# One load per chunk and two heads side by side in the rows of the array, in a fused retention and mixture-of-experts kernel

## The chip, the cores and the metric

The kernel runs on one core of a Trainium2 chip. The metric is the device time of one execution in microseconds (us); of several runs the median is given. Everything is read from one execution that the hardware profiler recorded. The engines are PE (TensorE, with PEld for its weight loads), DVE (VectorE), ACT (ScalarE), POOL (GpSimd) and SP (SyncE, which here issues the plain DMAs).

## The reference

Retention (a linear attention with a decaying state) over batch 4, 8 heads, 768 positions, head size 64, and behind it a mixture of 8 experts with top-1 routing over 3072 tokens of 512 features:

```python
for t in range(S):
    state = gamma * state + einsum('bhd,bhe->bhde', k[:, :, t], v[:, :, t])
    y[:, :, t] = scale * einsum('bhd,bhde->bhe', q[:, :, t], state)
x = y.transpose(0, 2, 1, 3).reshape(B * S, H * D)
logits = x @ w_gate;  expert_idx = argmax(logits);  gate_w = softmax(logits)[expert_idx]
for e in range(E):
    out[expert_idx == e] = gate_w * (relu(x @ w1[e]) @ w2[e])
```

## The kernel before

**Chunks.** The retention is computed in 24 chunks of 128 positions (6 per batch element), all eight heads at once, as four pairs of heads. For chunk `g` the kernel forms scores (key chunk times query chunk, masked to be causal), the output within the chunk (scores times values) and the carried part (queries times the state accumulated up to the chunk before). The decay is moved onto the operands: values are scaled by `cv` (negative powers of gamma), and queries or results by the table `G` (positive powers). The loop over `g` is written out in program order, one engine queue each, with no scheduler; only semaphores between engines hold things up.

**One pass of the loop** issues, in this order: `scores(g+1)`, `carry(g)`, `scale(g+2)`, for chunks 9 to 17 pieces of `split` (the weights of expert 0 cut into a high and a low part, ACT line 133, DVE or POOL line 134), `logits` of an earlier pair of chunks, `update(g)`, one or two stages of the routing of the batch element before (`gating`: `choose`, `soft`, `rank`, `slots`, `onehots`, `table`, `put_ids`, `weights`, `put_weights`), `output(g)`, the loads for chunk `g+4`, the store of a pair of chunks, and in four places a 1 MB weight load (`fetch`, line 125).

- `scale` (lines 207 to 215), POOL: from chunk 6 on, the queries times `G` in place (line 210); for every chunk the values times `cv` (line 212). For chunks below 6 `G` for that chunk is still being built (line 489, POOL, once per pass), and the result is multiplied instead (line 267, DVE).
- `scores` (217 to 226), PE line 222: for each half `h2` (the even or the odd head of the pairs) and each pair `p`, one matmul over all 128 rows. The moving operand holds the two heads' queries in the two row halves; the stationary operand `kt` holds one head's transposed keys in its row half and zeros in the other. So eight 128-row matmuls make the scores of eight heads, 64 rows of each being zeros. DVE line 224 masks the result into `Sb`, once per half.
- `carry` (244 to 250), PE line 249: four 128-row matmuls with the state of two heads as a block diagonal in `ub` (zeros off it).
- `update` (228 to 242), PE line 237: eight matmuls of 64 output rows each into the two halves of the partitions; ACT line 242 copies the state into `ub`, in two copies for the two diagonal blocks.
- `output` (252 to 272), PE line 257: eight matmuls, each 64 columns wide on the array, alternating between the two column halves. Then ACT line 269 copies `Y` to `xT` (DVE line 267 for chunks below 6), and DVE line 271 transposes it to `xn` for the store.
- `load` and `load_k` (193 to 202), SP: the three parts q, v, k of a chunk in one DMA of 768 KB, and the transposed keys as two DMAs of 128 KB, each into one row half of `kt`. `ld` has four buffers, `kts` four tiles; the loads of chunk `g+4` go where chunk `g` was.

**After the retention** PE computes an early half of expert 0 (`early_half`, `fill`), then all experts in `moe_main`. `L` (logits) has a PSUM bank of its own, `Y` one, the scores two.

A load in the program has this form, and the chunk's parts lie in memory as q, v, k and transposed k:

```python
nc.sync.dma_start(out=kts[g % 4][half[i], i], in_=qkv[g][half[i], 3].rearrange("a (p t) -> a p t", p=NP))
```

Of the kernel before, what the change touches and what calls it, by code (L numbers as in the profile page):

```python
# [43 lines left out]
G6 = CPB  # L44
BIG = 1 << 20
# [49 lines left out]
def retention_moe(ctx, tc, qkv, wg, w1, w2, cst, gdec, ustr, out):  # L95
# [75 lines left out]
    with ExitStack() as actx:  # L171
        apool = lambda name, bufs, **kw: actx.enter_context(tc.tile_pool(name=name, bufs=bufs, **kw))
        ld = apool("ld", 4)
# [10 lines left out]
        ubs = [ubp.tile([P, NP, P], F32, name=f"ub{i}") for i in range(3)]  # L184
        kts = [ubp.tile([P, 2, NP, C], F32, name=f"kt{i}") for i in range(4)]
# [3 lines left out]
        RAW = CPB  # L189
# [3 lines left out]
        def load(g, *parts):  # L193
            if g not in qs:
                qs[g] = ld.tile([P, 3, DM], F32, name="qkv_t", tag="ld")
            for part in parts or (slice(0, 3),):
                nc.sync.dma_start(out=qs[g][:, part], in_=qkv[g][:, part])

        def load_k(g):
            for i in range(2):  # L200
                nc.sync.dma_start(out=kts[g % 4][half[i], i],
                                  in_=qkv[g][half[i], 3].rearrange("a (p t) -> a p t", p=NP))

        def q_(g):
            return qs[g][:, 0].rearrange("a (p t) -> a p t", p=NP)

        def scale(g):
            c = g % CPB
            if g >= RAW:
                nc.gpsimd.tensor_tensor(out=q_(g), in0=q_(g), in1=G[:, c], op=ALU.mult)  # L210
            vs = wk.tile([P, H, D], F32, name="vs", bufs=3)
            nc.gpsimd.tensor_tensor(  # L212
                out=vs, in0=qs[g][:, 1].rearrange("a (h d) -> a h d", d=D),
# [3 lines left out]
        def scores(g):  # L217
            Sb = wk.tile([P, 2, NP, C], F32, name="Sb")
            for h2 in range(2):
                sp = ps_s.tile([P, NP, C], F32, name="sp")  # L220
                for p in range(NP):
                    nc.tensor.matmul(out=sp[:, p, :], lhsT=kts[g % 4][:, h2, p, :], rhs=q_(g)[:, p, :],  # L222
                                     start=True, stop=True)
                nc.vector.tensor_tensor(out=Sb[:, h2], in0=sp,
                                        in1=causal.unsqueeze(1).broadcast_to([P, NP, C]), op=ALU.mult)
            Sbs[g] = Sb

        def update(g):
# [4 lines left out]
            kn = qs[g][:, 2]  # L233
            for p in range(NP):
                for h2 in range(2):
                    r = slice(h2 * D, (h2 + 1) * D)
                    nc.tensor.matmul(out=U[r, p, :], lhsT=kn[:, p * P + h2 * D:p * P + h2 * D + D],
                                     rhs=vp[:, p, r], start=(c == 0 and p == 0), stop=True, skip_group_check=True)
            ub = ubs[g % 3]
            for h2 in range(2):  # L240
                r = slice(h2 * D, (h2 + 1) * D)
                nc.scalar.copy(out=ub[r, :, r], in_=U[r, :, :])

        def carry(g):
            c = g % CPB
            Y = Ys[g] = ps_1.tile([P, NP, C], F32, name="Y", tag="Y")
            if c > 0:
                for p in range(NP):
                    nc.tensor.matmul(out=Y[:, p, :], lhsT=ubs[(g - 1) % 3][:, p, :], rhs=q_(g)[:, p, :],
                                     start=(p == 0), stop=False, skip_group_check=True)  # L250

        def output(g):
            c = g % CPB
            Y, vp, Sb = Ys[g], vss[g], Sbs[g]
            for p in range(NP):
                for h2 in range(2):
                    nc.tensor.matmul(out=Y[h2 * D:(h2 + 1) * D, p, :],
                                     lhsT=vp[:, p, h2 * D:(h2 + 1) * D], rhs=Sb[:, h2, p, :],
                                     start=(c == 0 and p == 0), stop=True, skip_group_check=True)
# [6 lines left out]
            if g < RAW:  # L266
                nc.vector.tensor_tensor(out=xT, in0=Y, in1=G[:, c], op=ALU.mult)
            else:
# [747 lines left out]
```

## Time and profile before

| what | value |
|---|---|
| three runs | 447.74, 450.02, 451.33 us; median 450.02 |
| profiled execution, span from the first to the last instruction | 447.8 us |
| busy over the span | PE 419.0, DVE 284.4, ACT 148.0, POOL 293.0 us |
| mean granted PE clock | 0.979 of full speed |
| retention (up to the end of the last `output`) | 140.5 us |
| moved by DMA | 79.68 MB, of it 27.71 MB from 10 to 100 us |

The time of the profiled execution outside its span was not recorded for it; the span alone lies at the lowest of the three runs. The views used further on are: a table of busy time per engine in chosen stretches (with the granted clock, the DMA engines' busy share and GB/s), groups of instructions by line (busy time, mean ns of one, idle time ahead of them and what ended it), waits by who waited for whom, the instructions in order of time, and the DMA view. A busy PE need not be PE at its peak, as matmuls overlap.

### The profile page before, as it was taken

The numbers are of one execution on the slowest core, as the hardware profiler recorded it, in microseconds if no ns is written. First come the engines' busy times: TensorE is split into PE (matmuls) and PEld (weight loads), VectorE is DVE, ScalarE is ACT, GpSimd is POOL, SyncE is SP. The second block draws the span as 40 slices with busy tenths as digits, with TensorE's granted clock in tenths as the row PEclk, the third lists the DMA queues.
The fourth block names the chain that finished last, engine by engine and source line by source line (L and its number), as shares of the span: only waits on it lengthen the run. The fifth ranks groups of instructions, "written<-read, shape, count | busy, mean of one in ns | idle before, by whom it ended". The sixth has DMA issues, their size and how long they took to land. (4 is left out here: it accounts for less than half of the span.)

```text
span 447.8 us, 8078 instructions
## 1 busy us (share of the span) xinstructions
PE 419.0 (94%) x3085; PEld 388.3 (87%) x3085; DVE 284.4 (64%) x504; ACT 148.0 (33%) x259; POOL 293.0 (65%) x268
## 2 busy tenths in 40 slices
PE   8879979978999999999999999999999999999990
PEld 5868868867888989789999999999999999999860
DVE  5536888989875864578647738647757666666210
ACT  1011344431234313554234424415424424523100
POOL 2445557576871677778737878778877778776720
PEclk9989999996999999999999999999999999999996
DMA  6999999995943027376515443644553462531110
GB/s 197 313 278 285 293 317 310 337 322 175 278 130 76 21 70 242 122 266 226 214 57 198 162 135 136 233 136 135 183 191 117 177 212 102 188 124 37 53 49 18
DMA packets 46555, 79.68 MB, mean 178 GB/s; under 512 B 7147, under 2 KB 19823, under 8 KB 46514
## 3 DMA queue, kind: packets, MB, share of 16 engines
q1 hardware_dynamic: 39938, 65.76, 45.5%
q0 software_dynamic: 6576, 13.39, 9.0%
q8 instruction: 25, 0.41, 0.4%
q14 instruction: 16, 0.13, 0.1%
HBM read 66.52 MB, written 13.34 MB: 178 GB/s over the span
## 5 line engine op out<-in xcount | busy, mean ns | idle before, releaser
L650 POOL DMA_INDIRECT buf<-x_dram,gidx x92 | 101.8, 1107 | 28.0 <-issue 24.1
L641 POOL DMA_INDIRECT out<-Z,sidx x80 | 90.6, 1133 | 32.4 <-issue 21.0
L134 DVE TENSOR_TENSOR wlo<-raw,whi 128x1024 fp32r<-128x1024 f32 (+1 forms) x64 | 75.5, 1180 | 13.9 <-ACT whi L133 13.6
L133 ACT CAST whi<-raw 128x1024 fp32r<-128x1024 f32 (+1 forms) x72 | 67.4, 949 | 7.7 <-DMA raw<-w 7.6
L853 PE MATMUL py<-hh,whi 128*128 128x452 f32 (+5 forms) x192 | 67.0, 349 | 0.0
L853 PE MATMUL py<-hh,wlo 128*128 128x452 f32 (+5 forms) x192 | 66.9, 348 | 0.0
L853 PE MATMUL py<-hl,whi 128*128 128x452 f32 (+5 forms) x192 | 66.9, 348 | 0.0
L831 ACT ACTIVATE hh<-ph 128x256 fp32r<-128x256 f32 (+7 forms) x64 | 31.4, 491 | 88.0 <-PE ph L826 87.4
L832 DVE SCALAR_TENSOR_TENSOR hl<-ph,hh 128x256 fp32r<-128x256 f32 (+7 forms) x64 | 35.3, 554 | 35.1 <-ACT hh L831 34.5
L222 PE MATMUL sp<-qkv_t,kt 128*128 128x128 f32 x384 | 52.6, 295 | 4.6 <-DMA kt<-qkv 3.5
L222 PEld LDWEIGHTS sp<-qkv_t,kt 128*128 128x128 f32 x384 | 49.1, 207 | 7.8 <-issue 2.9
L826 PE MATMUL ph<-xh,whi 128*128 128x452 f32 (+6 forms) x224 | 50.3, 346 | 0.9 <-ACT xh L666 0.8
L826 PE MATMUL ph<-xh,wlo 128*128 128x452 f32 (+6 forms) x224 | 50.1, 345 | 0.0
L826 PE MATMUL ph<-xl,whi 128*128 128x452 f32 (+6 forms) x224 | 50.0, 345 | 0.0
L210 POOL TENSOR_TENSOR qkv_t<-qkv_t,buf 128x512 f32<-128x512 f32 x18 | 23.6, 1312 | 31.0 <-DMA qkv_t<-qkv 30.9
L826 PEld LDWEIGHTS ph<-xh,whi 128*128 128x128 f32 x224 | 40.6, 188 | 2.5 <-ACT xh L666 1.3
L826 PEld LDWEIGHTS ph<-xh,wlo 128*128 128x128 f32 x224 | 40.7, 188 | 0.8
L826 PEld LDWEIGHTS ph<-xl,whi 128*128 128x128 f32 x224 | 40.7, 188 | 0.7
L212 POOL TENSOR_TENSOR vs<-qkv_t,cs 128x512 f32<-128x512 f32 x24 | 26.9, 1119 | 20.9 <-DMA qkv_t<-qkv 18.4
L853 PEld LDWEIGHTS py<-hl,whi 128*128 128x128 f32 x192 | 36.1, 188 | 0.8
L853 PEld LDWEIGHTS py<-hh,whi 128*128 128x128 f32 x192 | 36.1, 188 | 0.8
L853 PEld LDWEIGHTS py<-hh,wlo 128*128 128x128 f32 x192 | 36.1, 188 | 0.7
(151 smaller groups left out, 608.4 us busy)
## 6 DMA issues: line engine op xcount, KB each, us to landing
raw<-w SPq DMA_DIRECT2D x32, 1024.0 KB, 5.0
qkv_t<-qkv SPq DMA_DIRECT2D x20, 768.0 KB, 8.7
kt<-qkv SPq DMA_DIRECT2D x48, 128.0 KB, 6.7
x_dram<-xn SPq DMA_DIRECT2D x48, 128.0 KB, 4.9
qkv_t<-qkv SPq DMA_DIRECT2D x8, 256.0 KB, 5.0
buf<-x_dram,gidx POOLq DMA_INDIRECT x92
out<-Z,sidx POOLq DMA_INDIRECT x80
qkv_t<-qkv SPq DMA_DIRECT2D x2, 512.0 KB
```

What stands on the lines that cost most here:

```text
L133: nc.scalar.copy(out=hi[:, h], in_=raw[:, h])
L134: engine.tensor_tensor(out=lo[:, h], in0=raw[:, h], in1=hi[:, h].bitcast(F32), op=ALU.subtract)
L210: nc.gpsimd.tensor_tensor(out=q_(g), in0=q_(g), in1=G[:, c], op=ALU.mult)
L212: nc.gpsimd.tensor_tensor(out=vs, in0=qs[g][:, 1].rearrange("a (h d) -> a h d", d=D), in1=cv[:, c, :].unsqueeze(2).broadcast_to([P, H, D]) ...
L222: nc.tensor.matmul(out=sp[:, p, :], lhsT=kts[g % 4][:, h2, p, :], rhs=q_(g)[:, p, :], start=True, stop=True)
L641: sc = tc.nc.gpsimd.indirect_dma_start(out=out, out_offset=bass.IndirectOffsetOnAxis(ap=index, axis=0), in_=rows, in_offset=None, bounds_c ...
L650: nc.gpsimd.indirect_dma_start(out=xg[:, j, :], out_offset=None, in_=x_slices, in_offset=bass.IndirectOffsetOnAxis(ap=index[:, j:j + 1], a ...
L826: nc.tensor.matmul(out=ph[:, :cap], lhsT=wparts[e, f // 4][a][:, kd, fo:fo + P], rhs=x[:, kd, :cap], start=(n == 0), stop=(n == 3 * KD - 1))
L831: nc.scalar.activation(out=hh[:, :cap], in_=ph[:, :cap], func=AF.Relu)
L832: nc.vector.scalar_tensor_tensor(out=hl[:, :cap], in0=ph[:, :cap], scalar=0.0, in1=hh[:, :cap].bitcast(F32), op0=ALU.max, op1=ALU.subtract)
L853: nc.tensor.matmul(out=py[:, :cap], lhsT=a[:, f % 4, k * P:(k + 1) * P], rhs=x[:, :cap], **se)
```

## The change

- **Scores by row halves.** The zero-padded `kt` tiles are gone. The stationary operand of each head is its 64 rows of the transposed keys, and the moving operand the same 64 rows of the queries; the even head uses array rows 0 to 63, the odd head rows 64 to 127, and they write to two PSUM banks. The loop runs over pairs first, so that the two row halves alternate.
- **Carried part by four 64x64 products.** `ub` holds only the diagonal blocks (64 columns instead of 128, no zeros to set). Each pair's two heads use the two row halves, and the pairs `2m` and `2m+1` the two column halves. `Y` now has two banks, one per row half, and half of each is used. To make room, `L` uses the bank of `mt` (the last one that of `misc`).
- **Order of features.** In `Y`, `xT` and the stored x, partition halves now stand for the pair's parity and the free dimension for row half and `m`. The host lays out `w_gate` and `w1` in the same order (`reordered`); nothing is computed there.
- **One load.** The parts lie as q, transposed k, v, k, and a chunk is one DMA of 1 MB (two of 512 KB for chunks 0 and 1). The loads run five chunks ahead, with five buffers.
- **Decay on the queries for every chunk.** `scale` multiplies the queries by `G` from chunk 0 on (chunk 0 on DVE, others on POOL); `G` of chunk `c` is built in `scale` by `grow`. ACT copies `Y` to `xT` for every chunk, and the transpose always reads `xT`.
- ACT copies the state in one instruction instead of two.

```diff
-        ubs = [ubp.tile([P, NP, P], F32, name=f"ub{i}") for i in range(3)]
-        kts = [ubp.tile([P, 2, NP, C], F32, name=f"kt{i}") for i in range(4)]
+        ubs = [ubp.tile([P, NP, D], F32, name=f"ub{i}") for i in range(3)]
...
+        def load(g, part=slice(0, 4)):
             if g not in qs:
+                qs[g] = ld.tile([P, 4, DM], F32, name="qkv_t", tag="ld")
+            nc.sync.dma_start(out=qs[g][:, part], in_=qkv[g][:, part])
...
         def scale(g):
             c = g % CPB
-            if g >= RAW:
-                nc.gpsimd.tensor_tensor(out=q_(g), in0=q_(g), in1=G[:, c], op=ALU.mult)
+            if g == c and g > 0:
+                grow(c)
+            engine = nc.vector if g == 0 else nc.gpsimd
+            engine.tensor_tensor(out=turned(g, 0), in0=turned(g, 0), in1=G[:, c], op=ALU.mult)
...
-            for h2 in range(2):
-                sp = ps_s.tile([P, NP, C], F32, name="sp")
-                for p in range(NP):
-                    nc.tensor.matmul(out=sp[:, p, :], lhsT=kts[g % 4][:, h2, p, :], rhs=q_(g)[:, p, :],
+            sps = [ps_s.tile([P, NP, C], F32, name="sp") for _ in range(2)]
+            for p in range(NP):
+                for r in range(2):
+                    nc.tensor.matmul(out=sps[r][:, p, :], lhsT=kt[half[r], p, :], rhs=q[half[r], p, :],
                                      start=True, stop=True)
...
-            for h2 in range(2):
-                r = slice(h2 * D, (h2 + 1) * D)
-                nc.scalar.copy(out=ub[r, :, r], in_=U[r, :, :])
+            nc.scalar.copy(out=ubs[g % 3], in_=U)
...
+                for m in range(2):
+                    for o in range(2):
+                        p = 2 * m + o
+                        for r in range(2):
+                            nc.tensor.matmul(out=Y[half[o], r, m * C:(m + 1) * C], lhsT=ubs[(g - 1) % 3][half[r], p, :],
+                                             rhs=q[half[r], p, :], start=(m == 0), stop=False, skip_group_check=True)
...
-        load(0, 0)
-        load_k(0)
+        load(0, slice(0, 2))
+        nc.sync.dma_start(out=G[:, 0], in_=gdec)
         nc.sync.dma_start(out=cs[:, 0:NFIRST], in_=cst[:, 0:NFIRST])
-        load(0, 1, 2)
+        load(0, slice(2, 4))
...
-            if g + 4 < NCH:
-                load(g + 4)
-                load_k(g + 4)
+            if g + AHEAD < NCH:
+                load(g + AHEAD)
```

PE, one pass of the loop (chunk 3 with its `output`, from `scores(4)` on): before,

```order
L222 MATMUL sp<-qkv_t,kt_125 128x128 x8
L249 MATMUL Y<-qkv_t,ub_124 128x128 x4
L283 MATMUL L<-xT,wgs 32x256 x4
L237 MATMUL U<-vs,qkv_t 64x64 x8
L257 MATMUL Y<-Sb,vs 64x128 x8
L295 MATMUL lp<-cs,LT 128x128 x2
```

and with the change:

```order
L223 MATMUL sp<-qkv_t 128x128 x8
L252 MATMUL Y<-qkv_t,ub_124 64x128 x8
L287 MATMUL L<-xT,wgs 32x256 x4
L238 MATMUL U<-vs,qkv_t 64x64 x8
L262 MATMUL Y<-Sb,vs 64x128 x8
L299 MATMUL lp<-cs,LT 128x128 x2
```

The order of the groups stays; the carried part has eight products for four, the scores read one tile for two. (The rows count matmuls of the program; the profile has two records for each of these, so 16 for 8.)

POOL, from the first values on (`vs` is line 212, the table `buf` is `G`, `qkv_t<-qkv_t` the queries): before,

```order
L212 TENSOR_TENSOR vs<-qkv_t,cs 128x512 x3
L489 TENSOR_TENSOR buf<-buf,cs 128x512
L212 TENSOR_TENSOR vs<-qkv_t,cs 128x512
L489 TENSOR_TENSOR buf<-buf,cs 128x512
L212 TENSOR_TENSOR vs<-qkv_t,cs 128x512
```

and with the change:

```order
L212 TENSOR_TENSOR vs<-qkv_t,cs 128x512
L201 TENSOR_TENSOR buf<-buf,cs 128x512
L210 TENSOR_TENSOR qkv_t<-qkv_t,buf 128x512
L212 TENSOR_TENSOR vs<-qkv_t,cs 128x512
L201 TENSOR_TENSOR buf<-buf,cs 128x512
L210 TENSOR_TENSOR qkv_t<-qkv_t,buf 128x512
```

For chunks 1 to 5 the table and the queries now stand ahead of the values of their chunk, and the scores of the chunk wait for them.

SP, the first DMAs: before,

```order
L197 DMA qkv_t<-qkv 128x512
L201 DMA kt_125<-qkv 64x512 x2
L439 DMA cs<-cst 128x200
L197 DMA qkv_t<-qkv 128x512 x3
L201 DMA kt_126<-qkv 64x512 x2
L197 DMA qkv_t<-qkv 128x512
L444 DMA buf<-gdec 128x512
```

and with the change:

```order
L195 DMA qkv_t<-qkv 128x1024
L439 DMA buf<-gdec 128x512
L440 DMA cs<-cst 128x200
L195 DMA qkv_t<-qkv 128x1024 x3
L195 DMA qkv_t<-qkv 128x2048 x3
```

The table `G` moved from behind the loads of chunk 1's values to the second place, and each chunk has one or two DMAs where it had three to five.

More of the change, by code (lines that the diff above doesn't have):

```diff
@@ L44 @@
 G6 = CPB
+AHEAD = 5
 BIG = 1 << 20
@@ L254, in output @@
             Y, vp, Sb = Ys[g], vss[g], Sbs[g]
[L255 to L259, printed above, removed]
+            for m in range(2):
+                for r in range(2):
+                    for o in range(2):
+                        p = 2 * m + o
+                        nc.tensor.matmul(out=Y[half[o], r, m * C:(m + 1) * C], lhsT=vp[:, p, half[r]],
+                                         rhs=Sb[:, r, p, :], start=(c == 0 and m == 0), stop=True,
+                                         skip_group_check=True)
             if g in logits_at:
@@ L265, in output @@
             xT = xTs[g // 2][:, :, (g % 2) * C:(g % 2 + 1) * C]
[L266 to L269 removed]
+            nc.scalar.copy(out=xT.rearrange("a (r m) t -> a r m t", m=2),
+                           in_=Y[:, :, 0:2 * C].rearrange("a r (m t) -> a r m t", m=2))
             xn = xns[g // 2][:, (g % 2) * 4:(g % 2 + 1) * 4]
             nc.vector.transpose(out=xn.rearrange("a j p c -> a p j c"),
[L272 removed]
+                                in_=xT.rearrange("a p (j r) -> a p j r", r=32))
         def store(t):
@@ L432, in fill @@
             state["half"] += n
-        for t in kts:
-            for i in range(2):
-                nc.vector.memset(t[half[1 - i], i], 0.0)
-        load(0, 0)
-        load_k(0)
-        nc.sync.dma_start(out=cs[:, 0:NFIRST], in_=cst[:, 0:NFIRST])
-        load(0, 1, 2)
-        load(1, 0)
-        load_k(1)
-        load(1, 1)
-        nc.sync.dma_start(out=G[:, 0], in_=gdec)
-        load(1, 2)
-        for g in (2, 3):
-            load(g, 0)
-            load_k(g)
-            load(g, slice(1, 3))
+        load(0, slice(0, 2))
+        nc.sync.dma_start(out=G[:, 0], in_=gdec)
+        nc.sync.dma_start(out=cs[:, 0:NFIRST], in_=cst[:, 0:NFIRST])
+        load(0, slice(2, 4))
+        load(1, slice(0, 2))
+        load(1, slice(2, 4))
+        for g in range(2, AHEAD):
+            load(g)
         warm = ps_m.tile([P, 512], F32, name="warm", tag="mt")
@@ L463, in retention_moe @@
         nc.sync.dma_start(out=x_dram[0:1, :], in_=zrow[0:1].rearrange("a j p c -> a (j p c)")[:, 0:DM])
-        for u in ubs:
-            nc.gpsimd.memset(u, 0.0)
         scale(0)
@@ L1000, in natural, with reordered @@
         return a.transpose(0, 2, 3, 1, 4).reshape(B, CPB, P, DM)
+    def reordered(a, axis):
+        a = np.asarray(a)
+        s = a.shape
+        a = a.reshape(*s[:axis], 2, 2, 2, D, *s[axis + 1:])
+        n = axis
+        order = [*range(n), n + 2, n, n + 1, *range(n + 3, a.ndim)]
+        return np.ascontiguousarray(a.transpose(order).reshape(s))
     cst, gdec, ustr = _constants()
     arrays = {
-        "qkv": np.stack([transposed(q), natural(v), natural(k), transposed(k)], axis=3).reshape(NCH, P, 4, DM),
-        "wg": np.ascontiguousarray(moe_w_gate), "w1": np.ascontiguousarray(moe_w1),
+        "qkv": np.stack([transposed(q), transposed(k), natural(v), natural(k)], axis=3).reshape(NCH, P, 4, DM),
+        "wg": reordered(moe_w_gate, 0), "w1": reordered(moe_w1, 1),
         "w2": np.ascontiguousarray(moe_w2), "cst": cst, "gdec": gdec, "ustr": ustr,
```

51 lines of the change are left out of this document (20 added, 31 removed).

## The prediction

> **What bounds the kernel now.** First I cut the span where the work changes, at the ends of the outputs of chunks 6, 12, 17 and 23, and read the table of stretches. Its columns are length, busy time of PE, PE's weight loads, DVE, ACT and POOL (with counts), granted clock, DMA share and GB/s.
>
> ```profile
> 5.30:45.60 40.30, 36.62 (x405) 32.57 (x406) 20.75 (x38) 5.70 (x16) 17.74 (x17) 0.96 0.97 286
> 45.60:77.20 31.60, 28.63 (x362) 25.22 (x363) 27.02 (x55) 12.78 (x28) 17.72 (x16) 1.00 0.98 309
> 77.20:114.70 37.50, 31.62 (x370) 27.97 (x371) 32.78 (x62) 12.67 (x28) 24.78 (x20) 0.91 0.89 278
> 114.70:140.50 25.80, 24.33 (x302) 21.63 (x302) 20.25 (x48) 8.66 (x20) 16.23 (x16) 1.00 0.57 158
> 140.50:180.00 39.50, 39.50 (x293) 35.62 (x294) 25.13 (x71) 13.44 (x31) 25.99 (x27) 1.00 0.35 109
> 180.00:430.00 250.00, 249.06 (x1327) 240.42 (x1327) 153.56 (x222) 93.49 (x136) 186.91 (x166) 1.00 0.44 153
> ```
>
> The first four rows are the retention, A to D below. PE is the busiest engine in all of them, but two others stand close behind: the DMA engines are busy 0.97 and 0.98 of A and B, and DVE 27.02 of 31.60 us in B and 32.78 of 37.50 in C. From 140.5 us on PE works without a gap, on experts that the change does not touch. So what the retention gains is handed on whole, and the question is how much of PE's saving DVE and the DMAs let through.
>
> Who waits for whom says the same from the other side (us in total, times, longest). PE, to 140.5 us:
>
> ```profile
> PE T L386 <- DVE vgw L404: 5.6, 3, 3.0
> PE sp L222 <- DMA kt<-qkv: 3.5, 3, 2.5
> PE pf L349 <- DVE EA L339: 2.0, 2, 1.0
> PE Y L249 <- DVE xn L271: 1.8, 1, 1.8
> ```
>
> DVE, from 45.6 to 140.5 us:
>
> ```profile
> DVE xn L271 <- ACT xT L269: 5.9, 5, 1.7
> DVE lg L299 <- PE lp L295: 5.4, 6, 1.7
> ```
>
> PE waits for routing steps on DVE (`vgw`, `EA`), and DVE's own waits lead back to PE's results, `xn` by way of ACT's copy of `Y`. A faster PE shortens the last two rows and lengthens the first and third.
>
> **What the change takes from PE.** The groups up to 140.5 us:
>
> ```profile
> L222 PE MATMUL sp<-qkv_t,kt 128*128 128x128 f32 x384 | 52.6, 295 | 4.6 <-DMA kt<-qkv 3.5 <-POOL qkv_t L210 0.9
> L249 PE MATMUL Y<-qkv_t,ub 128*128 128x128 f32 x160 | 21.6, 278 | 2.5 <-DVE xn L271 1.8 <-DVE xT L267 0.7
> L257 PE MATMUL Y<-Sb,vs 128*64 128x128 f32 x384 | 27.0, 283 | 0.0
> L237 PE MATMUL U<-vs,qkv_t 128*64 128x64 f32 x320 | 13.7, 228 | 0.0
> L283 PE MATMUL L<-xT,wgs 128*32 128x256 f32 x88 | 7.0, 391 | 0.0
> L237 PEld LDWEIGHTS U<-vs,qkv_t 128*64 128x64 f32 x320 | 10.9, 137 | 5.8 <-issue 4.1 <-POOL vs L212 0.7
> ```
>
> L222 and L257 have as many records (384) with equally wide moving operands, yet L257 takes 27.0 us and L222 52.6: L257's products use half the array's columns and run two at a time. Four column quarters run together in L283 (88 records of twice the width in 7.0 us). No row shows two row halves together. Bounds for the new scores: 27.0 us if they pair as column halves do, 52.6 if not at all. I take 27.0, from the nearest row: saved 25.6 us. The carried part becomes 320 records on quarter arrays: at L283's rate halved for width, 0.040 us each, 12.8 us; at L257's 0.070, 22.5. I take 13, saved 8.6 (other end: lost 0.9).
>
> [...] The PEld row has 320 loads of 64 columns in 10.9 us, 0.034 each, while one takes 137 ns: they overlap across halves. [...]
>
> Added on PE are changes of array shape, scores to carried part and, in chunks with `lp`, back. Their price is in the order of time:
>
> ```profile
> 37.68 1.95 PE L222 MATMUL sp<-qkv_t,kt 128*128 128x128 f32 x16
> 39.47 1.06 PE L249 MATMUL Y<-qkv_t,ub 128*128 128x128 f32 x8
> 40.45 1.09 PE L257 MATMUL Y<-Sb,vs 128*64 128x128 f32 x16
> 41.48 2.05 PE L222 MATMUL sp<-qkv_t,kt 128*128 128x128 f32 x16
> 43.46 0.64 PE L283 MATMUL L<-xT,wgs 128*32 128x256 f32 x8
> ```
>
> The first L222 hands over to L249, of the same shape: 39.47 - 37.68 = 1.79 us for 16, 0.112 each. L249's 8 would then fill 0.90 and fill 0.98 with a change behind them; the second L222 fills 1.98 with changes on both sides. So one costs 0.1 to 0.2 us. At 1.5 more per chunk: 24 x 1.5 x 0.15 = 5.4 us. PE's net saving is 25.6 + 8.6 - 5.4 = 28.8 us, 1.2 per chunk; bounds 34 and minus 6.
>
> **The other engines' part.** These rows price it (two groups to 140.5 us, then the DMA view from 10 to 100 us):
>
> ```profile
> L212 POOL TENSOR_TENSOR vs<-qkv_t,cs 128x512 f32<-128x512 f32 x24 | 26.9, 1119 | 20.9 <-DMA qkv_t<-qkv 18.4 <-PE Y L257 2.5
> L210 POOL TENSOR_TENSOR qkv_t<-qkv_t,buf 128x512 f32<-128x512 f32 x18 | 23.6, 1312 | 31.0 <-DMA qkv_t<-qkv 30.9
> L489 POOL TENSOR_TENSOR buf<-buf,cs 128x512 f32<-128x512 f32 x5 | 5.2, 1041 | 0.0
> L267 DVE TENSOR_TENSOR xT<-Y,buf 128x512 f32<-128x512 f32 x6 | 4.1, 687 | 6.6 <-DMA buf<-gdec 2.9 <-PE Y L257 2.5 <-POOL buf L489 1.1
> L242 ACT COPY ub<-U 64x256 f32<-64x256 f32 x40 | 14.6, 365 | 22.5 <-PE U L237 22.1
> ...
> DMA packets 16624, 27.71 MB, mean 308 GB/s; under 512 B 1993, under 2 KB 9440, under 8 KB 16613
> qkv_t<-qkv SPq DMA_DIRECT2D x17, 768.0 KB, 8.7
> ```
>
> POOL gains five query products, 5 x 1.312 = 6.6 us, all in A, where it is busy 17.74 of 40.30; for chunks 1 to 5 table, queries and values take 1.041 + 1.312 + 1.119 = 3.47 us per chunk, and behind them on POOL's queue stand the next chunk's, for which PE's scores wait. DVE loses six products (4.1 us) in A and gains one. ACT saves 20 copies, 7.3 us, hidden in any case: in B it works 12.78 of 31.60 us; were that cover gone, it would be a gain of 7.3. The wait of `carry` for `xn` (1.8 us) goes, as the transpose no longer reads `Y`; what comes next late there is ACT's copy. DMA bytes stay: 1.05 MB a chunk and 0.26 MB stored. A load's 8.7 us from issue to landing is the sign of a full queue, for the weight loads after 180 us take 5.0 for more bytes:
>
> ```profile
> raw<-w SPq DMA_DIRECT2D x25, 1024.0 KB, 5.0
> ```
>
> A fifth buffer does not empty the queue; one large load for three may help it a little. Slices of the same stretch reached more than the mean:
>
> ```profile
> GB/s 361 291 313 268 349 282 312 298 392 130 315 273 270 266 293 283 276 287 251 338 326 291 368 227 336 375 302 415 211 328 286 390 418 262 302 309 382 383 259 293
> ```
>
> So bounds of 308 and 360 GB/s; I take 308 to 330, nearer the mean.
>
> DVE's own work is not quite fixed. A step of the same kind and size took 1.31 us beside a POOL product and 0.52 without one:
>
> ```profile
> 99.08 1.04 POOL L212 TENSOR_TENSOR vs<-qkv_t,cs 128x512 f32<-128x512 f32 x1
> 99.18 1.31 DVE L404 TENSOR_TENSOR vgw<-ohi,gp 128x216 bf16<-128x216 bf16 x1
> 101.77 0.52 DVE L404 TENSOR_TENSOR vgw<-ohi,gp 128x216 bf16<-128x216 bf16 x1
> ```
>
> POOL's share in B rises only from 17.72/31.60 = 0.56 to 0.60, so I add nothing to DVE for it.
>
> **The sum, stretch by stretch**, against the profiled span of 447.8 us.
>
> A. PE needs 28.63/6 = 4.8 us per chunk in B, after the change 3.6; POOL 3.5; the DMAs 1.31 MB at 308 to 330 GB/s, 4.0 to 4.25. So the DMAs set 4.2 us. The first output ends later than now, for the queries of chunk 0 wait for `G` and one product: 0.69 us.
>
> ```profile
> 9.54 1.36 PE L257 MATMUL Y<-Sb,vs 128*64 128x128 f32 x16
> ```
>
> From 9.54 + 1.36 + 0.6 = 11.5 us, six chunks at 4.2 and 1 us for a slow clock at the start give 37.7 instead of 45.6: minus 7.9 (bounds 4 and 11).
>
> B. PE's floor falls to 28.63 - 6 x 1.2 = 21.4 us; DVE's stays at 27.02. Now DVE binds. Of its 4.6 idle us I leave 2.5, since three round trips to PE per batch element (`EA` to `pf`, `olo` to `T`, `vgw` to `T`) remain: 29.5, minus 2.1 (bounds 0 and 4.6).
>
> C. DVE 32.78, idle 3.0: 35.8, minus 1.7 (bounds 0 and 4.7). D. DVE 20.25, idle 2.5: 22.75, minus 3.1 (bounds 0 and 5.5).
>
> The rest: PE without gaps, nothing. Moved SBUF pools could cost or save a microsecond there. Sum 7.9 + 2.1 + 1.7 + 3.1 = 14.8 us, so a span of 433. The span lies 2.2 us below the median of the runs, 450.0; on that scale the change comes out at **435 us**, with its own range 428 to 442. Of 28.8 us saved on PE, half shows.
>
> The idle that I leave DVE has a reason in the clock:
>
> ```profile
> 97.70:101.10 3.40, 1.59 (x28) 1.02 (x27) 3.33 (x5) 1.10 (x3) 3.25 (x3) 1.00 1.02 287
> 101.10:107.90 6.80, 5.56 (x36) 5.07 (x36) 5.95 (x13) 1.62 (x3) 4.14 (x5) 0.50 0.63 213
> ```
>
> A stretch of 3.4 us in which PE was busy only 1.59 us (it waited for `vgw`) was followed by 6.8 us at half clock. With PE faster, each of the three `vgw` waits grows from at most 3.0 to about 4 us, and each may bring such a phase; in it a chunk takes PE 7.2 us against DVE's 4.5, some 2 us for DVE per event. [...]
>
> **Rivals.**
> *DMA-bound, 444 us.* From 10 to 100 us the queue is full; if 308 GB/s is a ceiling, the 27.71 MB there take 90 us again, and only what lies behind 100 us pays, C's last part and D, about 4 us, and 2 at the start. For it: shares of 0.97 and 0.98. Against it: PE waited for a DMA's landing only 3.5 us in all, and the slices above the mean.
> *No pairing, 446 us.* If row halves run one after the other, the change does not do what it says: PE saves at most the carried part less the shape changes, 3 us, and A's loads give 2. For it: no row shows row halves. Against it: the rows of column halves.
> *PE through, 424 us.* DVE idles nowhere and loads come at 360 GB/s: all upper bounds, 11 + 4.6 + 4.7 + 5.5 = 25.8. Against it: the round trips.
> *Half clock, slower, 458 us.* PE's new duty is 21.4 of 29.5 us in B; if its gaps are spread so that most stretches are half empty, the clock stays at 0.50. PE then needs 2 x (28.63 + 31.62 + 24.33 - 17 x 1.2) = 128 us for B to D, 94.9 now. At a half clock for four fifths of the time it is 107, 12 us worse, A's gain falls to 4: 458. It decides from about 0.7 of the time on. For it: the two rows above. Against it: a slow PE is a busy PE, and the clock came back after 6.8 us.
>
> **How the numbers follow.** Chances: forecast 0.64, DMA-bound 0.14, no pairing 0.09, PE through 0.07, half clock 0.06. A run of this kernel tells about 1% from no change, 4.5 us. Faster by more than that, below 445.5: forecast, PE through, DMA-bound but for 0.02, and 0.03 of no pairing: 0.86. Within 1%: the rest of these, 0.08. Slower: 0.06. The range reaches from 425 to 446, which leaves out the half clock and the edges of two others.
>
> **What would show it.** Right: scores near 27 us and the carried part near 13 by line; ends of the outputs at about 38, 67, 103 and 126 us; DVE above 0.9 busy in B and C with PE waiting for `vgw` 4 us at a time and three or four half-clock phases. Wrong: scores above 45 us (no pairing); DMA share 1.0 with POOL waiting for loads and DVE below 0.85 in B (DMA-bound); a clock mean below 0.7 in B to D (half clock).

## The result and the profile after

| | before | after |
|---|---|---|
| median of four runs each, same chip | 450.54 us | 437.65 us |
| lowest and highest | 447.74, 451.33 | 436.55, 438.73 |
| span of the profiled execution | 447.8 us | 437.0 us |
| last output of the retention ends at | 140.5 us | 128.4 us |

The ratio is 0.974, with an interval of 0.970 to 0.979. Forecast were 435 us and a ratio of 0.967. Medians here and below are over all executions of a kernel, and ratios compare only those within 1.5% of its fastest; three profiles below (loads cut as before, low parts on POOL, all three edits together) are of executions 1.5 to 2.2% above it.

The ends of the outputs of chunks 6, 12, 18 and 23 cut the retention into the same four stretches as in the prediction (A to D; the prediction says 17 for the third, but 114.7 us is the end of chunk 18; times in us, read from the rows of `output` in the order of time):

| | A, to chunk 6 | B, to 12 | C, to 18 | D, to 23 | behind it |
|---|---|---|---|---|---|
| ends before | 45.6 | 77.2 | 114.7 | 140.5 | 447.8 |
| ends after | 36.0 | 67.2 | 101.3 | 128.4 | 437.0 |
| change of the stretch | -9.6 | -0.4 | -3.4 | +1.3 | +1.3 |
| forecast | -7.9 | -2.1 | -1.7 | -3.1 | 0 |

This is the table of stretches of the kernel after (length, busy PE, weight loads, DVE, ACT and POOL with their counts, granted clock, DMA share, GB/s), A to D:

```profile
5.30:36.00 30.70, 26.33 (x445) 20.94 (x445) 16.30 (x28) 6.86 (x15) 24.18 (x22) 1.00 1.02 384
36.00:67.20 31.20, 25.55 (x404) 20.34 (x403) 27.26 (x55) 10.77 (x23) 20.11 (x17) 0.89 0.96 344
67.20:101.30 34.10, 26.06 (x410) 20.35 (x411) 30.72 (x62) 10.57 (x23) 20.43 (x17) 0.90 0.85 296
101.30:128.40 27.10, 22.27 (x342) 17.65 (x342) 20.34 (x49) 7.02 (x16) 17.17 (x17) 0.87 0.44 116
```

Read the last two columns against those of before. The DMA engines are about as busy in A as they were (1.02 now, 0.97 before), but move 384 GB/s where they moved 286. Length times rate gives the bytes: 30.7 us x 384 = 11.8 MB in A after, 40.3 x 286 = 11.5 MB before. About as many bytes came in three quarters of the time. B holds 10.7 MB now and 9.8 before, C 10.1 and 10.4, D 3.1 and 4.1: about 36 MB in all both times.

The groups up to the end of the retention (busy us, mean ns | idle before, with its releasers):

```profile
L223 PE MATMUL sp<-qkv_t 64*128 64x128 f32 x384 | 32.1, 309 | 4.5 <-DVE qkv_t L210 2.3 <-POOL qkv_t L210 2.1
L223 PEld LDWEIGHTS sp<-qkv_t 64*128 64x128 f32 x384 | 27.1, 210 | 10.3 <-issue 3.7 <-POOL qkv_t L210 3.3 <-DVE qkv_t L210 3.2
L252 PE MATMUL Y<-qkv_t,ub 64*64 64x128 f32 x320 | 14.3, 297 | 0.3 <-ACT xT L271 0.3
L262 PE MATMUL Y<-Sb,vs 128*64 128x128 f32 x384 | 29.7, 303 | 0.0
```

The row halves pair: scores went from 52.6 to 32.1 us, the carried part from 21.6 to 14.3. The unchanged products of L262 rose from 27.0 to 29.7, in stretches with a granted clock of 0.87 to 0.90, so a part of all three is the clock; the run below with a granted clock of 1.00 gives the rest (L262 takes 26.7 us there). PE's waits in the same time (total, times, longest):

```profile
PE T L390 <- DVE vgw L408: 6.7, 3, 3.3
PE pf L353 <- DVE EA L343: 6.2, 3, 2.5
PE T L390 <- DVE olo L384: 3.0, 1, 3.0
...
PE sp L223 <- POOL qkv_t L210: 2.1, 2, 1.2
```

PE now waits longer for the routing on DVE, as was to be expected of a faster PE; the loads have left the list (before, the scores waited 3.5 us for `kt`). What POOL waited for, to 46 us before and to 36 us after:

```profile
POOL vs L212 <- DMA qkv_t<-qkv: 18.4, 6, 5.7
POOL qkv_t L210 <- DMA qkv_t<-qkv: 7.3, 2, 4.8
```

```profile
POOL vs L212 <- DMA qkv_t<-qkv: 7.4, 1, 7.4
POOL qkv_t L210 <- DMA qkv_t<-qkv: 2.2, 2, 1.3
```

Before, six chunks' values were waited for, up to 5.7 us each; after, one. That points to the loads. It is no proof, for POOL had less to do before, and PE itself waited only 3.5 us for loads there.

So two theories stood. **Load form**: one DMA of 1 MB over all 128 partitions moves data faster than one of 768 KB and two of 128 KB over 64 partitions each, and A (with part of B and C) is as long as its transfers. **PE**: the 28.8 us that PE was to save are what A and C gained, and the loads merely followed a faster consumer. A third was about what is left: **half clock**, which should eat what B and D did not give.

### The profile page after: what moved, and what is told of

Its sections match the earlier page's. It is cut to its first block, busy times and chain, and to the rows that moved or that the text cites. A ratio compares the mean times of both kernels' runs of the same rounds, so it can differ in the third digit from the quotient of the medians.

```text
span 437.0 us, 8276 instructions
## 1 busy us (share of the span) xinstructions
PE 398.0 (91%) x3245; PEld 360.2 (82%) x3245; DVE 279.3 (64%) x491; ACT 143.4 (33%) x245; POOL 298.5 (68%) x270
## 5 line engine op out<-in xcount | busy, mean ns | idle before, releaser
L639 POOL DMA_INDIRECT buf<-x_dram,gidx x92 | 102.1, 1110 | 28.0 <-issue 27.1
L630 POOL DMA_INDIRECT out<-Z,sidx x80 | 91.7, 1146 | 32.3 <-issue 20.4
L135 DVE TENSOR_TENSOR wlo<-raw,whi 128x1024 fp32r<-128x1024 f32 (+1 forms) x64 | 79.0, 1236 | 16.6 <-ACT whi L134 16.3
L223 PE MATMUL sp<-qkv_t 64*128 64x128 f32 x384 | 32.1, 309 | 4.5 <-DVE qkv_t L210 2.3
L223 PEld LDWEIGHTS sp<-qkv_t 64*128 64x128 f32 x384 | 27.1, 210 | 10.3 <-issue 3.7
L226 DVE TENSOR_TENSOR Sb<-sp,cs 128x512 f32<-128x512 f32 x48 | 30.6, 676 | 6.5 <-PE sp L223 6.0
## 6 DMA issues: line engine op xcount, KB each, us to landing
x_dram<-xn SPq DMA_DIRECT2D x48, 128.0 KB, 4.0
```

Source lines behind the costliest of these rows:

```text
L135: engine.tensor_tensor(out=lo[:, h], in0=raw[:, h], in1=hi[:, h].bitcast(F32), op=ALU.subtract)
L223: nc.tensor.matmul(out=sps[r][:, p, :], lhsT=kt[half[r], p, :], rhs=q[half[r], p, :], start=True, stop=True)
L226: nc.vector.tensor_tensor(out=Sb[:, r], in0=sps[r], in1=causal.unsqueeze(1).broadcast_to([P, NP, C]), op=ALU.mult)
L630: sc = tc.nc.gpsimd.indirect_dma_start(out=out, out_offset=bass.IndirectOffsetOnAxis(ap=index, axis=0), in_=rows, in_offset=None, bounds_c ...
L639: nc.gpsimd.indirect_dma_start(out=xg[:, j, :], out_offset=None, in_=x_slices, in_offset=bass.IndirectOffsetOnAxis(ap=index[:, j:j + 1], a ...
```

## The experiments

Of the three chips on which the following kernels ran, two took some 50 us longer, the kernel before too; in the profiles that were kept the extra time lies behind the retention. So each time stands as a ratio to the kernel before on the same chip, and the end of the last output is given beside it. Why these chips were slower was not examined. The change itself was run again only on the faster chip, where "before" is 451.01 us; runs on the other two are compared with it by ratio and by the ends of their outputs.

| kernel | median us | before on that chip | ratio (interval) | last output ends |
|---|---|---|---|---|
| the change, again | 438.33 | 451.01 | 0.977 (0.970 to 0.985) | 129.3 |
| scores in series | 493.06 | 503.14 | 0.983 (0.974 to 0.992) | 128.0 |
| scores and carried part in series | 440.24 | 451.01 | 0.985 (0.976 to 0.994) | 130.9 |
| loads cut as before | 506.50 | 503.14 | 1.005 (0.999 to 1.010) | 150.6 |
| four loads of 256 KB | 446.89 | 451.01 | 0.997 (0.993 to 1.001) | 137.9 |
| two loads of 64 partitions | 468.27 | 451.01 | 1.044 (1.036 to 1.052) | 160.6 |
| before, with one load | 503.54 | 508.23 | 1.002 (0.996 to 1.008) | 140.6 |
| PE kept busy | 485.43 | 503.14 | 0.966 (0.959 to 0.973) | 127.9 |
| routing later | 488.55 | 503.14 | 0.973 (0.967 to 0.980) | 128.9 |
| tables of G on DVE | 491.94 | 508.23 | 0.980 (0.972 to 0.988) | 128.8 |
| low parts on POOL | 496.01 | 508.23 | 0.982 (0.973 to 0.992) | 137.2 |
| these last three together | 495.06 | 508.23 | 0.976 (0.968 to 0.985) | 135.5 |

### The change again

> The changed kernel itself, as a control beside the next three on one chip. Every theory: a ratio to the kernel before of 0.97 to 0.98, the last output of the retention at 127 to 130 us.

It repeats within the spread: ratio 0.977 beside 0.974, last output at 129.3 beside 128.4, 380 GB/s from 10 to 36 us beside 377.

### PE's saving taken back: scores in series

```diff
-            for p in range(NP):
-                for r in range(2):
+            for r in range(2):
+                for p in range(NP):
                     nc.tensor.matmul(out=sps[r][:, p, :], lhsT=kt[half[r], p, :], rhs=q[half[r], p, :],
```

> The changed kernel with the two loops of the scores exchanged, so that four products of one row half follow each other and then four of the other; all else as changed. Theory (row halves pair, and PE's saving reaches the end in part): the scores' busy time goes from 32.1 us to 45 to 52 us, and the time to 443 to 446 us. Rival (the single load carries the gain, PE's saving is lost in waits for VectorE): the scores get longer in the same way, and the time stays within 2 us of the changed kernel's 437.7 us. Rival (no pairing by order): the scores stay at 32 us, the time too.

The same products, but four of one row half in a row:

```profile
L223 PE MATMUL sp<-qkv_t 64*128 64x128 f32 x384 | 43.8, 298 | 2.3 <-DVE qkv_t L210 2.3
L223 PEld LDWEIGHTS sp<-qkv_t 64*128 64x128 f32 x384 | 39.0, 199 | 7.3 <-issue 3.3 <-DVE qkv_t L210 3.2 <-POOL qkv_t L210 0.5
```

The scores take 43.8 us, 11.7 more (45 to 52 us in all were expected), and the retention ends at 128.0 instead of 128.4. The ratio of the whole run, 0.983 with an interval of 0.974 to 0.992, is too wide to tell it from the change. In the order of time the loss is seen to come and go: chunk 6 ends at 38.2 (36.0 in the change), chunk 7 at 43.2 (43.3). PE was late by 2 us where it had nothing else to wait for, and caught up at the first wait.

That answers the question of pairing too: the order decides. Without alternation PE's weight loads are busy 39.0 us for 384 loads, 0.102 us each, with it 27.1 us, 0.071 each, while one load alone takes 199 and 210 ns: in alternation more of them overlap. With the row half the PSUM bank alternates as well in this kernel, and no run separates the two.

### Both in series

```diff
-                for m in range(2):
-                    for o in range(2):
-                        p = 2 * m + o
-                        for r in range(2):
+                for r in range(2):
+                    for o in range(2):
+                        for m in range(2):
+                            p = 2 * m + o
```

(in `carry`, beside the edit above)

> The changed kernel with the scores' loops exchanged as in the first experiment and the carried part's loops turned, so that products in the same quarter of the array follow each other. Theory now (the form of the load carries the gain, PE's saving is worth little): PE's scores and carried part take 15 to 20 us more than in the changed kernel, and the last output moves by less than 2 us, the ratio to the kernel before stays below 0.98. Rival (the first one, PE's saving carries half): the last output comes 5 to 8 us later, the ratio is 0.985 to 0.995.

```profile
10.00:36.00 26.00, 26.00 (x388) 22.00 (x386) 13.09 (x25) 6.12 (x13) 22.26 (x21) 1.00 1.01 375
```

PE is now busy in all of these 26 us, and the loads still come at 375 GB/s. Chunk 6 ends 2.0 us later than in the control (38.3 and 36.3), the retention 1.6 us later (130.9 and 129.3), the whole run 1.9. The scores took 44.8 us, 13.9 more than in the control, and the carried part 14.7 us where the control has 13.3: this order did not undo its pairing, and nothing here shows what the carried part in series would cost. So some 15 us of PE, half of what the change saves, cost about 2 us of time.

### The load form taken back

Three ways to cut the 1 MB of a chunk, everything else as in the change, the five buffers too. First much as before: queries, transposed keys in two halves of 64 partitions, values with keys. This is finer than the kernel before, which from chunk 4 on has queries, values and keys in one DMA of 768 KB.

```diff
-            nc.sync.dma_start(out=qs[g][:, part], in_=qkv[g][:, part])
+            if part.start == 0:
+                nc.sync.dma_start(out=qs[g][:, 0], in_=qkv[g][:, 0])
+                for i in range(2):
+                    nc.sync.dma_start(out=qs[g][half[i], 1], in_=qkv[g][half[i], 1])
+            if part.stop == 4:
+                nc.sync.dma_start(out=qs[g][:, 2:4], in_=qkv[g][:, 2:4])
```

> The changed kernel with its loads cut as before: queries, transposed keys in two row halves, values and keys, four DMAs per chunk; still five chunks ahead. Theory (PE's saving gives the most): DMA rate falls from 377 GB/s in the first 36 us to about 300 to 330, the first seven chunks take 3 to 5 us longer, the time is 440 to 442 us. Rival (the load form carries the gain): the retention's first part returns to 45 us and the time to 446 to 449 us.

```profile
10.00:36.00 26.00, 20.52 (x340) 16.66 (x340) 11.62 (x20) 5.53 (x12) 19.77 (x18) 0.91 1.02 274
```

The DMA engines are as busy as ever (1.02) and move 274 GB/s. The retention ends at 150.6, later than in the kernel before, with all of PE's saving in place. (The ratio of 1.005 says no faster than before.)

Second, four DMAs of 256 KB, all over 128 partitions, so that only the contiguous piece per partition shrinks, from 8 KB to 2 KB:

```diff
-            nc.sync.dma_start(out=qs[g][:, part], in_=qkv[g][:, part])
+            for i in range(part.start, part.stop):
+                nc.sync.dma_start(out=qs[g][:, i], in_=qkv[g][:, i])
```

> The changed kernel with a chunk's load cut into its four parts, each a DMA of 256 KB over all 128 partitions (2 KB per partition in one piece). Theory A (the DMAs into 64 partitions were what slowed the loads): the rate from 10 to 36 us stays at 350 to 377 GB/s and the last output at 128 to 131 us. Theory B (pieces of 2 KB are what slows them): the rate falls to 270 to 310 GB/s as with the cut loads before, and the last output comes at 140 to 150 us.

From 10 to 36 us, and B's place in the change; then the DMA view from 10 to 100 us:

```profile
10.00:36.00 26.00, 22.28 (x376) 17.40 (x375) 13.59 (x24) 5.75 (x12) 19.39 (x18) 0.96 0.93 297
36.00:67.20 31.20, 21.52 (x328) 16.94 (x329) 21.15 (x45) 7.43 (x17) 15.94 (x13) 0.78 1.00 319
```

```profile
DMA packets 22376, 28.63 MB, mean 318 GB/s; under 512 B 2340, under 2 KB 10629, under 8 KB 22363
```

Now 319 GB/s is what a full queue moves (share 1.00). Chunk 6 ends at 37.5, 1.2 us later than in the control; chunk 12 at 74.8, 7.2 later; chunk 23 at 137.9, 8.6 later. All that is different is the size of the pieces and, with it, the number of DMAs. This cut leaves 4.1 of the control's 12.7 us, and its interval includes no change.

Third, two DMAs with the large pieces of 8 KB, each over 64 partitions:

```diff
-            nc.sync.dma_start(out=qs[g][:, part], in_=qkv[g][:, part])
+            for r in half:
+                nc.sync.dma_start(out=qs[g][r, part], in_=qkv[g][r, part])
```

> The changed kernel with a chunk's load cut into two DMAs of 512 KB, one for partitions 0 to 63 and one for 64 to 127 (8 KB per partition in one piece). Theory A (DMAs into 64 partitions slow the loads): the rate from 10 to 36 us falls to 270 to 320 GB/s and the last output comes at 135 us or later. Theory B (the size of the pieces decides): rate and last output as in the changed kernel, 350 to 377 GB/s and 128 to 130 us.

```profile
10.00:36.00 26.00, 19.09 (x250) 15.66 (x250) 9.23 (x16) 4.20 (x9) 14.61 (x15) 0.71 1.03 219
36.00:67.20 31.20, 24.21 (x378) 18.82 (x379) 16.46 (x35) 5.66 (x13) 13.26 (x12) 0.89 1.04 248
```

```profile
DMA packets 10412, 21.71 MB, mean 241 GB/s; under 512 B 1453, under 2 KB 7288, under 8 KB 8484
qkv_t<-qkv SPq DMA_DIRECT2D x28, 512.0 KB, 12.3
```

Few, large packets, a share of 1.03, and 219 GB/s: a load of half a megabyte takes 12.3 us to land where the change's megabyte took 8.4. The scores wait for it by way of POOL's query product (to 128.4 us):

```profile
PE sp L224 <- POOL qkv_t L211: 16.4, 11, 3.9
```

The retention ends 31 us later than in the control and the run is 4% slower than before. So in these runs the number of partitions that one DMA spans weighs more than the size of its pieces: from 10 to 36 us 219 GB/s over 64 partitions in pieces of 8 KB, 297 over 128 in pieces of 2 KB. Later this kernel's rate is 248 GB/s (above) and, from 67.2 to 101.3 us, 255, in stretches that also hold 1 MB weight loads. Why loads over 64 partitions come more slowly, no run here shows.

Put in order, the runs with the new PE order show the end of the retention following the rate from 10 to 100 us: 342 GB/s and 129.3 us (control), 318 and 137.9, 279 and 150.6 (the first cut), 241 and 160.6. The kernel before, with the old PE order, had 308 and 140.5. A line between its two neighbours in this list gives 141.2 at 308 GB/s, as if PE's saving were worth nothing. That is weak, for a late kernel loads less by 100 us whatever made it late: with low parts on POOL (below), whose loads are those of the change, the rate is 329 GB/s and the end 137.2.

### The load form alone

The opposite test gives the kernel before one DMA per chunk. Its keys must lie zero-padded in memory then, so that a chunk has 1.25 MB and no DMA splits at 64 partitions; the host writes the zeros.

```diff
-                qs[g] = ld.tile([P, 3, DM], F32, name="qkv_t", tag="ld")
-            for part in parts or (slice(0, 3),):
-                nc.sync.dma_start(out=qs[g][:, part], in_=qkv[g][:, part])
-
-        def load_k(g):
-            for i in range(2):
-                nc.sync.dma_start(out=kts[g % 4][half[i], i],
-                                  in_=qkv[g][half[i], 3].rearrange("a (p t) -> a p t", p=NP))
+                qs[g] = ld.tile([P, 5, DM], F32, name="qkv_t", tag="ld")
+            nc.sync.dma_start(out=qs[g][:, part], in_=qkv[g][:, part])
...
```

> The kernel before with its loads alone changed: the host lays the transposed keys out with their zeros, and a chunk is one DMA of 1.25 MB over 128 partitions (two for chunks 0 and 1), four chunks ahead; TensorE's work as before, 25% more bytes loaded. Theory (DMAs into 64 partitions bound the kernel before): the rate from 10 to 36 us rises from 294 to 350 to 380 GB/s, which is a quarter more bytes in the same time or less; chunk 6 ends at 41 to 44 us instead of 45.6, the last output at 132 to 138 us instead of 140.5, the ratio to the kernel before is 0.98 to 1.0. Rival (TensorE bounds the kernel before): the last output stays at 140 to 142 us.

```profile
10.00:36.00 26.00, 23.99 (x292) 21.57 (x293) 16.04 (x27) 3.68 (x10) 12.86 (x13) 1.00 1.01 372
36.00:67.20 31.20, 26.10 (x334) 22.63 (x329) 26.51 (x49) 10.12 (x24) 16.25 (x15) 0.99 1.02 371
```

The rate is 372 GB/s with the old PE order: the rate belongs to the load form and not to a faster consumer. The time did not fall, against the expectation: the retention ends where it did (140.6 and 140.5). A fifth of each load is zeros, so the useful rate lies between 372 / 1.25 = 298 GB/s and, as the stores carry no zeros, about 310 (an estimate: 1.31 of 1.57 MB per chunk); the kernel before had 299 in the same window.

The first chunks did gain. Chunk 6 ends at 40.5 us, 5.1 earlier than before, where 41 to 44 was expected. From 24 to 40 us PE has no gap, and the DMA engines are hardly less busy:

```profile
24.00:40.00 16.00, 16.00 (x209) 13.77 (x210) 9.65 (x18) 2.92 (x8) 7.96 (x8) 1.00 0.98 331
```

So the load form alone brought about half of the 9.6 us of A. The other 4.5 us came only with the new PE order; whether the old order or the extra bytes stood in their way, this run can't tell. Behind chunk 6 the 5.1 us were lost again, 4.0 of them up to chunk 12 (35.6 us beside 31.6), where from 36 to 67.2 us the queue is full with a quarter more bytes to load. PE is busy there too, in 31.11 of the 34.10 us from 67.2 to 101.3. A version of the old order with one load and no extra bytes was not tried.

### The clock

Eight bf16 products of 512 columns, whose result nobody reads, stand ahead of the routing stages, so that PE has work while it waits for DVE:

```diff
+            if b > 0 and c in (1, 3, 4):
+                keep = ps_m.tile([P, 512], F32, name="keep", tag="mt")
+                for i in range(8):
+                    nc.tensor.matmul(out=keep, lhsT=ones, rhs=ones.unsqueeze(1).broadcast_to([P, 4, P]),
+                                     start=True, stop=True)
```

> The changed kernel with eight bf16 products of 512 columns into an unused PSUM bank, about 1.7 us, ahead of the three waits per batch element (rank, the two tables); nothing reads them. Theory (the half clock costs): the four half-clock phases, 20.5 us in all, vanish or halve, and the time falls by 2 to 4 us to 433 to 436 us. Rival (VectorE's throughput binds, the clock costs nothing): the phases vanish and the time stays at 437 to 439 us.

The change (B is the stretch 36.00 to 67.20 shown above; here in finer cuts), then this kernel:

```profile
36.00:60.00 24.00, 18.35 (x297) 14.77 (x295) 20.96 (x43) 6.78 (x15) 13.33 (x11) 0.89 1.04 374
60.00:90.00 30.00, 24.73 (x381) 19.17 (x380) 26.19 (x50) 11.61 (x25) 21.75 (x17) 0.86 0.91 323
```

```profile
36.00:60.00 24.00, 22.01 (x331) 15.37 (x327) 21.16 (x44) 6.96 (x16) 13.89 (x11) 1.00 1.03 365
60.00:90.00 30.00, 27.68 (x412) 19.50 (x409) 28.39 (x54) 11.81 (x25) 21.80 (x17) 1.00 0.95 339
101.30:128.40 27.10, 24.82 (x358) 17.77 (x355) 19.44 (x48) 7.58 (x17) 16.74 (x16) 1.00 0.40 109
```

Each set of eight took PE 1.90 us. The granted clock is 1.00 throughout; the 20.5 us at half clock are gone (before the change there were 10.2). The scores take 30.7 us, the carried part 13.3, L262's products 26.7. And the retention ends at 127.9, half a microsecond earlier. Half clock was there, and taking it away gained next to nothing. That PE was waiting anyway would explain it, but the products that fill the gaps also take PE time (22.01 us busy from 36 to 60 beside 18.35), and what they cost was not measured apart. The ratio of this kernel is the lowest of all, 0.966, but its interval overlaps that of the change; it is not shown to be faster.

### Attempts on what is left

Three edits by three ideas of what binds now: the routing stages issued behind `output` instead of ahead of it (PE's waits of 16 us for DVE); the tables of `G` on DVE (POOL binds A, with 24.18 of 30.70 us); all low parts of expert 0 on POOL (DVE binds B and C, with 27.26 of 31.20 and 30.72 of 34.10); and all three.

```diff
-            if b > 0:
-                for i in {1: (2, 3), 2: (4,), 3: (5, 6), 4: (8,)}.get(c, ()):
-                    stages[i]()
             output(g)
+            if b > 0:
+                for i in {1: (2, 3), 2: (4,), 3: (5, 6), 4: (8,)}.get(c, ()):
+                    stages[i]()
```

> The changed kernel with the routing steps of passes 1 to 4 of a batch element issued after output(g) instead of ahead of it, so that TensorE does the output and the logits' transposes before it waits for VectorE. Theory (round trips between TensorE and VectorE bind chunks 7 to 23): the waits for EA and vgw, 12.9 us, shrink by about 1.3 us each time, half-clock phases get fewer, and the time falls to 432 to 435 us. Rival (VectorE's throughput binds): PE waits elsewhere, the time stays at 436 to 439 us.

```diff
-            nc.gpsimd.tensor_tensor(
+            nc.vector.tensor_tensor(
                 out=G[:, c], in0=G[:, 0], op=ALU.mult,
```

> The changed kernel with the five tables G of chunks 1 to 5 made on VectorE instead of GpSimd. Theory (GpSimd, 22.1 of 26 us busy from 10 to 36 us, binds the first chunks): chunk 6 ends 2 to 3 us earlier, at 33 to 34 us, and the last output 1 to 3 us earlier. Rival (the DMAs bind there): chunk 6 stays at 35.5 to 36.5 us.

```diff
-split(0, *i, nc.gpsimd if i[1] % 2 == 0 else nc.vector, 1)
+split(0, *i, nc.gpsimd, 1)
```

> The changed kernel with the low parts of expert 0's weights all made on GpSimd (sixteen products of 128x512) instead of half on VectorE, which loses 8.1 us between chunks 9 and 17. Theory (VectorE's throughput binds there): the last output comes 3 to 6 us earlier, at 123 to 126 us, the ratio is 0.962 to 0.970. Rival (the round trips bind, or VectorE slows beside a busier GpSimd): the last output stays within 1.5 us of 128.4.

> The changed kernel with the two edits above and the routing steps behind the output: if VectorE's throughput binds, the last output at 120 to 124 us and a ratio of 0.955 to 0.965; if the round trips bind, 125 to 128 us and 0.968 to 0.975.

None gained. With the stages later, chunk 9 ends at 48.8 instead of 51.6, and chunk 23 at 128.9 instead of 128.4. With the tables on DVE POOL has 18.47 us of work from 10 to 36 instead of 22.10, and chunk 6 ends at 37.0, 0.7 later than the control: POOL does not bind A. With the low parts on POOL, the whole stretch from chunk 6 to chunk 23 (B to D) is the one to compare, as it holds the same work; first the change, then this kernel:

```profile
36.00:128.40 92.40, 73.88 (x1154) 58.34 (x1152) 78.32 (x164) 28.36 (x62) 57.71 (x49) 0.89 0.76 260
```

```profile
36.10:137.20 101.10, 78.60 (x1154) 61.47 (x1152) 81.70 (x156) 28.56 (x62) 66.48 (x57) 0.86 0.69 235
```

Eight instructions went from DVE (164 to 156) to POOL (49 to 57), and POOL's busy time rose by 8.8 us. DVE's did not fall by the 8.1 us that the eight took there; it rose by 3.4: some of what stayed on DVE took longer beside a busier POOL (the nine `vgw` steps 747 ns each, 520 in the change), and the retention ends at 137.2. All three together end at 135.5. One execution of each kernel was profiled, and how much of the delay belongs to the edits is not shown. As ratios the four lie between 0.973 and 0.982, not to be told from the change.

## Why the prediction was right in number, and only in part for its reason

**The number.** 437.65 us beside 435, inside its range of 428 to 442. The ends of the outputs were forecast as 38, 67, 103 and 126 us and came at 36.0, 67.2, 101.3 and 128.4. That the total is so near is in part luck: all five stretches were off, by 1.3 to 4.4 us, two of them one way and three the other.

**What PE saves: right.** Scores 27.0 forecast, 32.1 measured, 30.7 at full clock; carried part 13, and 14.3 or 13.3. At full clock scores, carried part and L262 take 30.7 + 13.3 + 26.7 = 70.7 us. They took 52.6 + 21.6 + 27.0 = 101.2 before, with some half clock in it, and 98.3 in the kernel before with one load: 27.6 to 30.5 saved, with the changes of shape in it, beside the net 28.8 of the sum. Where one row half follows itself, the scores took 43.8 and 44.8 us.

**What PE's saving is worth: not as the sum has it.** "Of 28.8 us saved on PE, half shows" took the gain for PE's, let through by DVE and the loads. Without the large loads hardly any of it showed: with the load cut into 256 KB the retention ended 2.6 us earlier than before, with the other two cuts later. With the large loads half of the saving could be given back for 1.6 us at the end of the retention and about 2 of the run. What the other half is worth is open: the large loads under the old PE order brought chunk 6 forward by 5.1 of the 9.6 us, and the rest of A may be PE's.

**The rate of the loads: the step that failed.** "One large load for three may help it a little", with 308 to 330 GB/s taken and 360 as the bound. Measured were 377 from 10 to 36 us and 340 from 10 to 100 us, and each of the three ways of cutting the load lost most or all of the gain. The form of the load was priced as bookkeeping, by the number of DMAs; what counted is the span of partitions (219 GB/s for 64, with pieces of 8 KB) and the size of the pieces (297 to 319 for 2 KB on 128). A quarter of each chunk came by DMAs of 64 partitions. An estimate from these rows, 768 KB at 380 and 256 KB at 219 GB/s, is 321 on average, somewhat above the 299 to 308 of the kernel before. A hint stood in the DMA view of before, in the row below the one that the prediction shows:

```profile
kt<-qkv SPq DMA_DIRECT2D x35, 128.0 KB, 7.4
```

128 KB over 64 partitions took 7.4 us to land, 768 KB over 128 took 8.7. Both times hold the wait in a full queue (share 1.00 from 10 to 100 us), so the row prices nothing by itself, but it asks a question that the prediction did not put.

**A, -7.9 forecast, -9.6 measured.** The pace of 4.2 us per chunk was met, (36.0 - 11.3) / 6 = 4.1, with two wrong factors: from 11.3 to 36.0 us 375 GB/s move 9.3 MB, 1.5 per chunk where 1.31 was taken, and they move faster. The microsecond for a slow clock was not needed (1.00 in A).

**B, -2.1 and -0.4: "Now DVE binds" is not what the runs show.** DVE is busy 27.26 of 31.20 us (0.87), the DMA share is 1.04 up to 60 us, and the edits that lengthened B most were those of the loads: with the 256 KB loads B took 37.3 us (37.5 to 74.8), with the other two cuts more. What DVE gave up to POOL bought nothing.

**C, -1.7 and -3.4; D, -3.1 and +1.3.** C came out better and D worse. In D the DMA share is 0.44 and PE has 4.8, DVE 6.8 us idle. In D's first chunk the routing loses 2.7 us in one step, `EA`; DVE in the order of time:

```profile
103.51 2.94 DVE L343 TENSOR_TENSOR EA<-eq,ed 128x48 bf16<-128x48 f32 x1
106.37 0.20 DVE L347 TENSOR_TENSOR sh<-lg,mx 128x48 f32<-128x48 f32 x1
```

The next step, with as many elements, takes 0.20 us, and the same `EA` took 0.21 in the batch element before, at 70.90 us. POOL in the same time:

```profile
103.14 0.94 POOL L639 DMA_INDIRECT xg<-x_dram,gidx  x1 [0.30 <-issue]
104.11 1.27 POOL L210 TENSOR_TENSOR qkv_t<-qkv_t,buf 128x512 f32<-128x512 f32 x1
105.33 1.04 POOL L212 TENSOR_TENSOR vs<-qkv_t,cs 128x512 f32<-128x512 f32 x1
```

`EA` ends at 106.45, as soon as POOL's two products are through (106.37), and PE waits for it. That POOL's products made `EA` wait is likely by these times, but no run took them away. And with a full clock, later stages or work moved off DVE, D did not get shorter (27.8, 29.2 and 30.0 us).

**Half clock: right in kind, wrong in price.** Four phases were there, of 3.3 to 6.9 us at a granted clock of 0.50 or 0.51, where three or four were forecast. But only one came with a wait for `vgw`, of 3.31 us where 4 was forecast; the others came with waits for `EA` (2.33 and 2.54) and `olo` (2.99), and waits for `vgw` of 1.35 and 2.01 us brought none. They were to cost DVE some 2 us each; taking all four away gave 0.5 us together, with the cost of the filling in it.

**The rivals.** "DMA-bound, 444 us" had the mechanism nearly right and the ceiling wrong: its 308 GB/s belonged to the loads as they were cut (340 from 10 to 100 us in the change). "No pairing" did not come true (its sum, 450 less 3 and 2, is 445 and not 446). The series, which undoes part of the pairing, cost 0 to 2 us; a full loss was not run. "Half clock, slower" fell with the result, a granted clock of 0.87 or more in every stretch.

**Open** stays what sets the last eight chunks, from about 90 us, where neither an engine nor the DMAs are full; how the gain divides between the loads and PE, as the one test of the old order of PE with full-rate loads carried a quarter more bytes; and what the fifth buffer is worth. The three cuts keep it and lose the gain, so it alone is not the cause.

## What to carry to other kernels

Where the DMA share stands near 1 in a stretch, read its GB/s as well, stretch by stretch: a full queue at 286 to 309 GB/s (A and B before, share 0.97 and 0.98) was not at its ceiling, and one load of 1 MB over 128 partitions in pieces of 8 KB made it 377. Before pricing a saving on the busiest engine, multiply rate by length and see whether the bytes or the engine fix the stretch; with the load in four parts, the whole saving on an engine at 0.9 left 4.1 us of the run. And a half clock behind a wait need not be worth what it seems: filling the gaps here took away all 20.5 us at half clock and gave 0.5 us of time, with the cost of the filling in it.

## What the hardware showed that was not expected

- **The span of partitions counted more than the size of the pieces.** Loads of 512 KB over 64 partitions with 8 KB pieces: 219 to 255 GB/s; of 256 KB over 128 partitions with 2 KB pieces: 297 to 327; of 1 MB over 128 with 8 KB pieces: 362 to 387 (10 to 36 us, nine profiles).
- **Row halves of the array paired better in alternation.** The same 384 products of 64 rows took 30.7 us alternating with the clock at 1.00 throughout (30.9 to 36.7 in the other runs) and 43.8 to 44.8 in series; with zero-padded 128 rows it was 50.9 to 52.6.
- **The clock fell after a short pause.** PE waited 2.33 us for `EA`, and the stretch from 40.9 to 44.3 us that follows was at 0.50; a wait of 2.01 us later on was followed by no such stretch:

```profile
38.70:41.00 2.30, 0.01 (x2) 0.04 (x1) 2.19 (x5) 0.00 (x0) 2.02 (x2) 0.98 1.10 364
40.90:44.30 3.40, 3.26 (x33) 2.91 (x34) 2.38 (x9) 1.09 (x3) 0.84 (x2) 0.50 1.00 388
```

- **With work moved from DVE to POOL, DVE was busier.** Eight instructions fewer, 8.1 us of work, and DVE was busy 81.70 us instead of 78.32, in one profiled execution of each. A small step of 0.2 us took 2.94 once, with POOL's products of 1.0 to 1.3 us beside it.
